# Building the third segment's output, and the last one's first octet, in the bank of P @ V instead of a bank borrowed from the maxima

## The chip, the cores and the metric

The kernel runs on one core of one Trainium2 chip. The metric is the device time in microseconds (us). The time before is the median of three runs; beside it stands one profiled execution, from which every duration in this document before the prediction is taken.

## The reference

Two attention layers over the same 2048 tokens are mixed by a gate that depends on the token:

```python
x = A_x                                             # 2048 x 512
g = sigmoid((x * gate_w).sum(-1, keepdims=True))
a = A_ref(x, A_wqkv, A_wo)       # 32 heads of 16, softmax over all 2048 keys, then @ wo
b = B_ref(x, B_wq, B_wk, B_wv, B_wo, B_beta)
                                 # 4 segments of 512 tokens: causal softmax inside the segment,
                                 # plus a memory of earlier segments, then @ wo
return g * a + (1 - g) * b
```

Everything is float32. Both layers end in a product with a 512 x 512 matrix, so the output rows of one block of 128 tokens are a sum over 2 sides x 4 groups of 8 heads ("octets"), each with K = 128.

## The kernel before, in words

**Segments and units.** The four segments of 512 query tokens are numbered 0 to 3. A unit is one side, four heads and one segment: side A has 8 units in each segment (all 2048 keys), side B also 8 (the segment's own keys). Units alternate A, B, A, B; at the very end the order is B, A (line 100). An A unit has 64 slots, a B unit 10. A slot is one 128 x 512 tile of scores: one matmul into a bank of `st` (line 615), one exp on ScalarE into a tile `p` (line 638). There are 2368 slots, 592 in a segment, 74 in a pair of an A and a B unit.

**Two passes.** The scores are made twice. 96 slots ahead of its exp (LEAD), a first product of the same size is made into a bank of `sm` (line 205) and VectorE takes the row maxima of it (line 220; B's diagonal blocks go by ScalarE, GpSimd and VectorE, lines 231 to 235). The maxima are transposed (line 195) and loaded into two rows of the q tile, so that the second product has them subtracted already. In every slot one score matmul and one matmul for the maxima are issued, in alternating halves of the array's rows. The last 96 slots have no maxima beside them.

**Banks of PSUM in the main stage (lines 567 to 573).** Three banks `st` for scores; four banks `sm0` to `sm3` for products of maxima, handed round through the list `free` (line 840); one bank `ops`, in which P @ V of one unit at a time is summed.

**Bursts.** The loop at line 831 issues three slots, then one burst of other work on TensorE. P @ V comes from a queue (line 598), into which four pieces of 128 columns go when their four exps are issued. A burst takes 3 pieces from it, or 4 when more than 6 wait (`MOST + (len(queue) > 6)`, line 851); neighbours of one tile are joined in a matmul of up to 512 columns, one for each of the four heads in its own 32 columns of the array (line 671). A piece is 128 columns. When a unit's last piece is done, ScalarE copies `ops` out (line 675) and a DMA stores it. The tiles `p` are six (`NP`, line 39), four slots each; a score may only be written over a tile whose P @ V is issued (line 609).

**The output product.** `octet` (line 701) loads eight stored heads back, scales them by the reciprocal of the sum, the gate and so on, some 28 slots later. `piece` (line 744) multiplies one scaled octet of one side with one quarter of the columns of `wo`: four matmuls of 128 columns side by side in the array. A block of 128 tokens has 32 pieces. They are issued in three ways:

- Segments 0 and 1 (`SHARED`): at the end of each A unit of the *next* segment, `half_block` (line 774) queues 16 pieces, half of the columns of one block, summed in `ops` itself. As long as there are any, a burst issues four of them in place of P @ V (line 847). ScalarE then copies 128 x 256 out (line 783).
- Segment 2: `block_fill` (line 758) takes a bank out of `free` and fills it with 32 pieces, one in each burst, behind that burst's P @ V (lines 856 to 859). Four blocks in turn; line 790 copies each out. The first octet of segment 3 (`keep`, 8 pieces a block, from slot nS - 208) goes the same way into tiles `part` (line 799). While a block is under way three banks are left for the maxima.
- The rest of segment 3 (`close`, line 818): one bank for each of the four blocks, two pieces in a burst once the maxima are over, `part` added at the end (line 868).

Pieces of the last two ways leave out a burst in which maxima are transposed (line 853).

Of the kernel before, what the change touches and what calls it, by code (L numbers as in the profile page):

```python
# [10 lines left out]
F32 = mybir.dt.float32  # L11
# [8 lines left out]
D = 512  # L20
# [3 lines left out]
NCH = S // CH  # L24
KT = D // 128
NG = 8
NO = 4
# [9 lines left out]
BURST = 3  # L37
MOST = 3
NP = 6
SHARED = (0, 1)  # L40
GAP = {"A": 3, "B": 5}
MASK_T = 8
LATE_T = 8
# [5 lines left out]
def gated_mix(ctx, tc, x, xT, wqkv, a_wo, b_wq, b_wk, b_wv, b_wo, beta, gate_w, out):  # L49
    nc = tc.nc  # L50
# [56 lines left out]
    seg_end = {(s, c): max(end[s, g, c] for g in range(NG)) for s in "AB" for c in range(NCH)}  # L107
    nS = len(slots)
# [4 lines left out]
    for k in range(NU):  # L113
# [4 lines left out]
        for p in range(64 + 10 * len(bs)):  # L118
            r = (len(maxs) + 1) % 2
            i = (p - start) // apart  # L120
# [131 lines left out]
    def run_todo(m):  # L252

        for e in [e for e in todo if e[0] <= m]:
            todo.remove(e)
            e[1]()
# [22 lines left out]
    with ExitStack() as p0:  # L279
# [22 lines left out]
        def post(slots, place, f):  # L302
            posted.setdefault((now[0] + slots, place), []).append(f)
# [163 lines left out]
        def mem_q(o, c, pq):  # L467
            nps = me_ps.tile([128, CH], F32, tag="me", name="num")
            nc.tensor.matmul(nps, mbd[o].rearrange("p e h -> p (e h)"), pq, start=True, stop=True)  # L469
            am = wk.tile([128, CH], F32, tag="am", name="am", bufs=1)  # L470
            nc.scalar.copy(am, nps)
            nc.sync.dma_start(numd[c][:, o], am)
            pqs.append(pq)
            if o == NO - 1:
                post(1, 1, lambda: mem_den(c))
# [13 lines left out]
        def mem_k(o, c, pk, vs):  # L489
            tps = me_ps.tile([128, 4, 128], F32, tag="me", name="tps")  # L490
            for b in range(4):
                nc.tensor.transpose(tps[:, b], pk[:, b * 128:(b + 1) * 128], identf)
            pt = wk.tile([128, 4, 128], F32, tag="pt", name="pt", bufs=1)
            nc.scalar.copy(pt, tps)
            post(0, 3, lambda: mem_k2(o, c, pt, vs))
# [36 lines left out]
        for c in range(NCH):  # L532
            for o in range(NO):
                then = (lambda pq, o=o, c=c: post(1, 1, lambda: mem_q(o, c, pq))) if c else None
# [5 lines left out]
            for o in range(NO):  # L540
                then = (lambda pk, o=o, c=c, vs=vs: post(1, 1, lambda: mem_k(o, c, pk, vs))) if c + 1 < NCH else None
# [24 lines left out]
    fr = ctx.enter_context(tc.tile_pool(name="fr", bufs=1, reuse_waits="tile"))  # L566
# [4 lines left out]
    banks = [sm_ps.tile([128, CH], F32, name=f"sm{i}") for i in range(4)]  # L571

    ops = o_ps.tile([128, CH], F32, name="ops")
# [4 lines left out]
    def load_wo(side, w):  # L578
        wos[side] = wo.tile([128, NO, D], F32, name=f"wo{side}")
        nc.sync.dma_start(wos[side], w.rearrange("(o p) d -> p o d", p=128))  # L580
# [17 lines left out]
    queue = []  # L598
# [51 lines left out]
    def some_values(n, most):  # L650

        while queue and most and queue[0][0] <= n:
            _, u, i = queue.pop(0)
            most -= 1
            side, g, c = u
            w = 1
            while (queue and most and queue[0][0] <= n and queue[0][1] == u and (i + w) // 4 == i // 4
                   and (side == "A" or PIECES[i + w][0] == PIECES[i][0])):
                queue.pop(0)
                most -= 1  # L660
                w += 1
            p = pt_[u, i // 4]
            if side == "A":
                c0 = q0 = 128 * (i % 4)
                v = vt[u][:, i // 16, i // 4 % 4]
            else:
                b, c0, q0 = PIECES[i]
                v = vt[u][:, b]
            done = i + w == SLOTS[side]
            for h in range(4):  # L670
                nc.tensor.matmul(ops[32 * h:32 * h + 17, q0:q0 + 128 * w], v[:, 17 * h:17 * h + 17], p[:, h, c0:c0 + 128 * w],  # L671
                                 start=(i == 0), stop=done, tile_position=(0, 32 * h))
            if done:
                raw = ob.tile([128, CH], F32, tag="o", name="oraw")
                nc.scalar.copy(raw, ops)
                nc.sync.dma_start(od[side, c][4 * g:4 * g + 4].rearrange("h r t -> (h r) t"), raw)
                stored.add(u)
                if side == "B" and c and g % 2 == 0:
                    octet("M", g // 2, c, n + 4)
                if (side, g ^ 1, c) in stored and u != ("A", NG - 1, NCH - 1):  # L680
                    octet(side, g // 2, c, n + 8)
                if side == "A" and c - 1 in SHARED:
                    shared.extend(half_block(c - 1, g // 2, g % 2))
                return


# [11 lines left out]
    def at(n, f):  # L698
        beside.setdefault(n, []).append(f)
# [44 lines left out]
    def piece(ps, side, o, c, b, j, start, stop):  # L744

        assert (side, o, c) in scaled
        for t in range(4):
            nc.tensor.matmul(ps[32 * t:32 * t + 32, 128 * (j % (ps.shape[1] // 128)):128 * (j % (ps.shape[1] // 128)) + 128],  # L748
                             held[side, c][:, o, 128 * b + 32 * t:128 * b + 32 * t + 32], wos[side][:, o, 128 * j:128 * j + 128],
                             start=start, stop=stop, tile_position=(0, 32 * t))  # L750

    def out_rows(c, b):
        return out[c * CH + b * 128:c * CH + (b + 1) * 128, :]

    fill = []
    lent = {}

    def block_fill(n, octets, c, b, then):

        ks = [(side, o) for o in octets for side in "AB"]  # L760
        for i in range(4 * len(ks)):
            def f(i=i):
                if i == 0:
                    lent[c, b] = free.pop(0)
                ps = banks[lent[c, b]]
                piece(ps, *ks[i // 4], c, b, i % 4, i == 0, i == 4 * len(ks) - 1)
                if i == 4 * len(ks) - 1:
                    then(ps)
                    free.append(lent[c, b])
            fill.append((n, f))  # L770

    shared = []

    def half_block(c, b, half):

        ps = ops[:, 0:256]
        ks = [(side, o) for o in range(NO) for side in "AB"]
        for i in range(16):
            def f(i=i):
                piece(ps, *ks[i // 2], c, b, 2 * half + i % 2, i == 0, i == 15)  # L780
                if i == 15:
                    t = fr.tile([128, D], F32, tag="res", name="res", bufs=2)
                    nc.scalar.copy(t[:, 0:256], ps)
                    nc.sync.dma_start(out_rows(c, b)[:, 256 * half:256 * half + 256], t[:, 0:256])
            yield f

    def leave(c, b):
        def then(ps):
            t = fr.tile([128, D], F32, tag="res", name="res", bufs=2)
            nc.scalar.copy(t, ps)  # L790
            nc.sync.dma_start(out_rows(c, b), t)
        return then

    part = {}

    def keep(b):
        def then(ps):
            part[b] = fr.tile([128, D], F32, tag=f"part{b}", name="part")
            nc.scalar.copy(part[b], ps)
        return then  # L800

    for u in units:
        at(max(0, first[u] - 30), lambda u=u: load_v(u))
    at(100, lambda: load_wo("A", a_wo))
    at(180, lambda: load_wo("B", b_wo))
    last = NCH - 1
    for c in range(NCH):
        if c < last and c not in SHARED:
            for b in range(4):
                block_fill(seg_end["A", c] + 24, range(NO), c, b, leave(c, b))  # L810
    for b in range(4):
        block_fill(nS - 208, range(1), last, b, keep(b))

    free = list(range(4))
    closing = [(side, o) for o in range(1, NO) for side in "BA"]
# [14 lines left out]
    n = 0  # L830
    while n < nS or queue or beside or filled[0] < len(fill):
        for f in beside.pop(n, []):
            f()
        if n < nS:
            score_part(n)
        m = n + LEAD
        if m < nS:
            loads(m + PRE)

            def bank():  # L840
                i = free.pop(0)
                free.append(i)
                return banks[i]
            max_part(m, bank)
        run_todo(m)
        if n % BURST == BURST - 1 or n >= nS:
            if shared:
                for _ in range(4):
                    shared.pop(0)()
            else:  # L850
                some_values(n, MOST + (len(queue) > 6) if n < nS else 8)

            if any(e[0] < m + 1 for e in late):
                run_late(st_ps, "st", m + 1)
            else:
                for _ in range(1 if m < nS else 2):
                    if filled[0] < len(fill) and fill[filled[0]][0] <= n:
                        fill[filled[0]][1]()
                        filled[0] += 1
        n += 1  # L860
    octet("A", NO - 1, last, None, vector=True)
    assert len(stored) == len(units)
    for b in range(4):
# [3 lines left out]
        t = fr.tile([128, D], F32, tag="res", name="res", bufs=2)  # L867
# [37 lines left out]
```

## Time and profile before

| | |
|---|---|
| median of 3 runs | 1941.87 us (1939.02 to 1943.77) |
| the profiled execution's own time | 1940.47 us |
| its span, first to last instruction | 1938.8 us |
| clock granted to TensorE, mean over the span | 0.993 |

By the starts of the score matmuls of line 615, the main stage goes from 345.1 us to 1913.4 us after the span's start. Segment 0's slots begin at 345.1, segment 1's at 727.4, segment 2's at 1109.8, segment 3's at 1493.6. "Stretch" below means a part of the span between two such times. Durations of neighbouring matmuls overlap in the profile, because matmuls are pipelined; the distance between the starts of two instructions is therefore used as the price of what lies between.

### The profile page before, as it was taken

Reading aid. Unit: us, or ns where it says so; the run is one execution under the profiler, and the core shown is the slowest. Engines: PE = TensorE matmul, PEld = TensorE weight load, DVE = VectorE, ACT = ScalarE, POOL = GpSimd, SP = SyncE. Lnnn points to the kernel's source line nnn. Section 1 sums busy time; section 2 is a strip of 40 time slices with the busy share of each in tenths; the row PEclk is TensorE's granted clock in tenths of the full one; section 3 lists DMA queues with packets and bytes.
Section 4 is the critical chain, followed back from the end, with each engine's and each line's share of the span. In section 5 each row is a group of like instructions: output and inputs, shape, how many; then the busy total and the mean of one; then the engine's idle time right before and its main releaser. Section 6 shows DMA issues by size and latency. Waiting matters only on the chain.

```text
span 1938.8 us, 44063 instructions
## 1 busy us (share of the span) xinstructions
PE 1897.4 (98%) x17009; PEld 993.5 (51%) x17009; DVE 1611.9 (83%) x2768; ACT 1467.0 (76%) x2859; POOL 281.7 (15%) x497
## 2 busy tenths in 40 slices
PE   7999999999999999999999999999999999999997
PEld 6888766444444444444444444444444455555545
DVE  4235687899999999999999999999999889889810
ACT  3234432788888888888888888888888787878874
POOL 3000000211111111121111111111111111111210
PEclk9999999899999999999999999999999999999999
DMA  6667645434233334343444344434334333333211
GB/s 204 204 228 254 201 155 166 114 101 133 85 107 84 107 85 119 91 117 91 118 93 116 103 105 104 104 105 107 105 104 105 101 93 102 101 105 96 80 53 40
DMA packets 123632, 227.16 MB, mean 117 GB/s; under 512 B 35064, under 2 KB 48920, under 8 KB 122912
## 3 DMA queue, kind: packets, MB, share of 16 engines
q1 hardware_dynamic: 121840, 223.24, 41.0%
q8 instruction: 135, 2.21, 0.5%
q0 software_dynamic: 1296, 0.59, 0.2%
q14 instruction: 73, 0.60, 0.1%
q10 hardware_dynamic: 288, 0.52, 0.1%
HBM read 155.52 MB, written 67.52 MB: 115 GB/s over the span
## 4 chain that ended last, share of the span: by engine, by line
PE 89%; DMA 3%; ACT 3%; DVE 3%; issue 1%; POOL 0%; SPq 0%; ACTq 0%; POOLq 0%; DVEq 0%
PE ops L671 30%; PE st L615 27%; PE sm L205 14%; PE pr L312 11%; PE ops L748 3%; PE sm L748 2%; ACT p L638 2%; DVE pm L220 1%; DMA qdA<-q 1%; PE num L469 1%; DMA kdB<-q 1%; PE mt_ps L195 1%; ACT dg L231 1%; PE mps L500 0%; DMA qdB<-q 0%
## 5 line engine op out<-in xcount | busy, mean ns | idle before, releaser
L638 ACT ACTIVATE p<-st 128x512 f32<-128x512 f32 x2304 | 1219.5, 605 | 205.8 <-PE sm L205 168.7
L220 DVE TENSOR_REDUCE pm<-sm 128x1 f32<-128x512 f32 x2048 | 1286.5, 682 | 94.1 <-PE sm L205 71.3
L205 PE MATMUL sm<-kA,qA 48*128 48x512 f32 x2048 | 757.7, 450 | 1.3 <-DVE pm L220 1.3
L615 PE MATMUL st<-qA,kA 50*128 50x512 f32 x2048 | 702.9, 439 | 7.8 <-ACT p L638 7.1
L671 PE MATMUL ops<-p,vA 128*17 128x512 f32 (+2 forms) x4912 | 561.2, 529 | 0.0
L615 PEld LDWEIGHTS st<-qA,kA 50*128 50x128 f32 x2048 | 336.1, 186 | 412.6 <-ACT p L638 336.9
L205 PEld LDWEIGHTS sm<-kA,qA 48*128 48x128 f32 x2048 | 338.3, 185 | 37.7 <-DVE pm L220 22.9
L205 PE MATMUL sm<-kB,qB 48*128 48x128 f32 (+2 forms) x896 | 171.5, 295 | 0.6 <-DVE pmB L241 0.5
L671 PEld LDWEIGHTS ops<-p,vA 128*17 128x17 f32 x4912 | 81.7, 95 | 165.0 <-issue 153.9
L205 PEld LDWEIGHTS sm<-kB,qB 48*128 48x128 f32 x896 | 135.0, 188 | 10.6 <-DVE pm L220 2.6
L232 POOL TENSOR_SCALAR_AFFINE_SELECT dg<-dg 128x512 f32<-128x512 f32 x128 | 81.2, 637 | 301.2 <-ACT dg L231 299.6
L615 PE MATMUL st<-qB,kB 50*128 50x384 f32 (+3 forms) x512 | 120.9, 342 | 3.3 <-ACT p L638 2.4
L360 DVE TENSOR_TENSOR q<-pr,q 128x512 fp32r<-128x512 f32 x64 | 44.0, 687 | 90.8 <-ACT q L353 78.3
L353 ACT CAST q<-pr 128x512 fp32r<-128x512 f32 x64 | 37.5, 585 | 99.3 <-PE pr L312 63.6
L188 POOL CAST ms<-nm 128x16 fp32r<-128x16 f32 x64 | 12.6, 197 | 650.5 <-DVE nm L181 392.5
L615 PEld LDWEIGHTS st<-qB,kB 50*128 50x128 f32 x512 | 72.6, 186 | 66.3 <-ACT p L638 52.0
L619 POOL TENSOR_SCALAR_AFFINE_SELECT p<-p 128x512 f32<-128x512 f32 x128 | 78.7, 634 | 95.6 <-ACT p L638 95.0
L671 PE MATMUL ops<-p,vB 128*17 128x512 f32 (+3 forms) x1024 | 89.2, 444 | 1.7 <-issue 1.5
L241 DVE TENSOR_REDUCE pmB<-sm 128x4 f32<-128x512 f32 x128 | 87.1, 681 | 1.2 <-PE sm L205 1.2
L235 DVE TENSOR_REDUCE pmB<-dg 128x4 f32<-128x512 f32 x128 | 86.7, 677 | 0.8 <-POOL dg L232 0.8
L231 ACT COPY dg<-sm 128x512 f32<-128x512 f32 x128 | 76.4, 597 | 1.8 <-DVE pmB L235 1.8
L722 DVE RECIPROCAL rec<-rec 128x32 f32<-128x32 f32 x44 | 15.1, 343 | 71.2 <-DMA rec<-odA 40.3
(129 smaller groups left out, 1567.5 us busy)
## 6 DMA issues: line engine op xcount, KB each, us to landing
kA<-kdA SPq DMA_DIRECT2D x256, 128.0 KB
vA<-vdA SPq DMA_DIRECT2D x32, 544.0 KB
kA<-kdA SPq DMA_DIRECT2D x256, 64.0 KB
qdA<-q SPq DMA_DIRECT2D x32, 256.0 KB
kdA<-q SPq DMA_DIRECT2D x32, 256.0 KB
qdB<-q SPq DMA_DIRECT2D x32, 256.0 KB
qA<-qdA SPq DMA_DIRECT2D x64, 128.0 KB
kdB<-q SPq DMA_DIRECT2D x32, 256.0 KB
```

The source lines that it names most:

```text
L205: nc.tensor.matmul(ps[:, n0:n0 + n], rows(qt[u][:, :, s * 128:(s + 1) * 128], h, 48), rows(k[:, :, k0:k0 + n], h, 48), start=True, stop=True)
L220: nc.vector.tensor_reduce(pm[:, h, s, kc:kc + 1], ps, axis=AX.X, op=ALU.max)
L231: nc.scalar.copy(dg, blocked(ps))
L232: nc.gpsimd.affine_select(out=dg, in_=dg, pattern=[[0, 4], [-1, 128]], base=0, channel_multiplier=1, compare_op=ALU.is_ge, fill=MASKED)
L235: todo.append((m + MASK_T, lambda: nc.vector.tensor_reduce(to, dg.rearrange("p (h s) t -> p h s t", h=2), axis=AX.X, op=ALU.max)))
L241: nc.vector.tensor_reduce(pm[:, 1, h, 3:7], blocked(ps), axis=AX.X, op=ALU.max)
L312: nc.tensor.matmul(ps, l(a, k), r(b, k), start=(n == 0), stop=(n == 11))
L615: nc.tensor.matmul(ps[:, n0:n0 + CH - q0], rows(k[:, :, b * 128:(b + 1) * 128], h, 50), rows(q[:, :, q0:], h, 50), start=True, stop=True)
L619: nc.gpsimd.affine_select(out=x, in_=x, pattern=[[0, 4], [1, 128]], base=0, channel_multiplier=-1, compare_op=ALU.is_ge, fill=0.0)
L638: nc.scalar.activation(p[:, h], ps, AF.Exp, scale=SCALE)
L671: nc.tensor.matmul(ops[32 * h:32 * h + 17, q0:q0 + 128 * w], v[:, 17 * h:17 * h + 17], p[:, h, c0:c0 + 128 * w], start=(i == 0), stop=done ...
L748: nc.tensor.matmul(ps[32 * t:32 * t + 32, 128 * (j % (ps.shape[1] // 128)):128 * (j % (ps.shape[1] // 128)) + 128], held[side, c][:, o, 12 ...
```

## The change

The whole of segment 2's output and the first octet of segment 3 leave the borrowed bank. `half_block`, `block_fill` and the numbers in `SHARED` become one generator `output(c, b, octets, cols, then)`, which sums in the first columns of `ops`, and a table `between` that says which unit's end starts which piece of output:

- at the end of each A unit of segments 1, 2 and 3 except the very last: half of the columns of one block of the segment before (16 pieces, four bursts of four), as segments 0 and 1 had it;
- at the ends of the first two B units of segment 3: one quarter each of the columns that the last A unit leaves over (8 pieces, two bursts);
- at the ends of the next four B units of segment 3: the first octet of one block of segment 3, all columns (8 pieces, two bursts), copied to `part`.

No bank is taken out of `free` any more before the closing pieces. A burst of P @ V now takes a fifth piece when more than 13 wait; this holds in all segments. `close` and the end of the kernel stay as they are.

```diff
-                if side == "A" and c - 1 in SHARED:
-                    shared.extend(half_block(c - 1, g // 2, g % 2))
+                if u in between:
+                    shared.extend(output(*between[u]))
...
-    def block_fill(n, octets, c, b, then):
-        ks = [(side, o) for o in octets for side in "AB"]
-        for i in range(4 * len(ks)):
-            def f(i=i):
-                if i == 0:
-                    lent[c, b] = free.pop(0)
-                ps = banks[lent[c, b]]
-                piece(ps, *ks[i // 4], c, b, i % 4, i == 0, i == 4 * len(ks) - 1)
-                if i == 4 * len(ks) - 1:
-                    then(ps)
-                    free.append(lent[c, b])
-            fill.append((n, f))
...
+    def output(c, b, octets, cols, then):
+        ps = ops[:, 0:128 * len(cols)]
+        ks = [(side, o, j) for o in octets for side in "AB" for j in cols]
+        for i, (side, o, j) in enumerate(ks):
+            def f(i=i, side=side, o=o, j=j):
+                piece(ps, side, o, c, b, j, i == 0, i == len(ks) - 1)
+                if i == len(ks) - 1:
+                    then(ps, c, b, cols)
             yield f
...
+    last = NCH - 1
+    between = {("A", g, c): (c - 1, g // 2, range(NO), range(2 * (g % 2), 2 * (g % 2) + 2), leave)
+               for c in range(1, NCH) for g in range(NG)}
+    del between["A", NG - 1, last]
+    for j in (2, 3):
+        between["B", j - 2, last] = (last - 1, 3, range(NO), (j,), leave)
+    for b in range(4):
+        between["B", b + 2, last] = (last, b, (0,), range(4), keep)
...
-    for c in range(NCH):
-        if c < last and c not in SHARED:
-            for b in range(4):
-                block_fill(seg_end["A", c] + 24, range(NO), c, b, leave(c, b))
-    for b in range(4):
-        block_fill(nS - 208, range(1), last, b, keep(b))
...
-                some_values(n, MOST + (len(queue) > 6) if n < nS else 8)
+                some_values(n, MOST + (len(queue) > 6) + (len(queue) > 13) if n < nS else 8)
```

More of the change, by code (lines that the diff above doesn't have):

```diff
@@ L39 @@
 NP = 6
-SHARED = (0, 1)
 GAP = {"A": 3, "B": 5}
@@ L755, in gated_mix @@
     fill = []
-    lent = {}
-    def block_fill(n, octets, c, b, then):
-        ks = [(side, o) for o in octets for side in "AB"]
-        for i in range(4 * len(ks)):
-            def f(i=i):
-                if i == 0:
-                    lent[c, b] = free.pop(0)
-                ps = banks[lent[c, b]]
-                piece(ps, *ks[i // 4], c, b, i % 4, i == 0, i == 4 * len(ks) - 1)
-                if i == 4 * len(ks) - 1:
-                    then(ps)
-                    free.append(lent[c, b])
-            fill.append((n, f))
@@ L772, in gated_mix @@
-    shared = []
[L774 to L784, printed above, removed]
-            yield f
@@ L787, in leave @@
[L787 to L792, printed above, removed]
-    part = {}
[L796 to L800, printed above, removed]
+    shared = []
+    def output(c, b, octets, cols, then):
[6 more added lines that the diff above has]
+                    then(ps, c, b, cols)
+            yield f
@@ new lines, in leave, with keep @@
+    def leave(ps, c, b, cols):
+        w, j0 = 128 * len(cols), 128 * cols[0]
+        t = fr.tile([128, D], F32, tag="res", name="res", bufs=2)
+        nc.scalar.copy(t[:, 0:w], ps)
+        nc.sync.dma_start(out_rows(c, b)[:, j0:j0 + w], t[:, 0:w])
+    part = {}
+    def keep(ps, c, b, cols):
+        part[b] = fr.tile([128, D], F32, tag=f"part{b}", name="part")
+        nc.scalar.copy(part[b], ps)
+    last = NCH - 1
+    between = {("A", g, c): (c - 1, g // 2, range(NO), range(2 * (g % 2), 2 * (g % 2) + 2), leave)
+               for c in range(1, NCH) for g in range(NG)}
@@ L805, in gated_mix @@
     at(180, lambda: load_wo("B", b_wo))
-    last = NCH - 1
-    for c in range(NCH):
-        if c < last and c not in SHARED:
-            for b in range(4):
-                block_fill(seg_end["A", c] + 24, range(NO), c, b, leave(c, b))
-    for b in range(4):
-        block_fill(nS - 208, range(1), last, b, keep(b))
     free = list(range(4))
```

## The prediction, made before the changed kernel was run

> **What bounds the kernel now.** The page comes first, then the span cut at the segments' borders.
>
> ```profile
> PE 1897.4 (98%) x17009; PEld 993.5 (51%) x17009; DVE 1611.9 (83%) x2768; ACT 1467.0 (76%) x2859; POOL 281.7 (15%) x497
> ...
> PEclk9999999899999999999999999999999999999999
> ```
>
> TensorE is busy almost everywhere, but its row counts pipelined matmuls; the stages say more. The view by stretches (columns: busy us of the engines, clock, DMA):
>
> ```profile
> core 0: us, PE busy (x) PEld busy (x) DVE busy (x) ACT busy (x) POOL busy (x), PEclk, DMA share, GB/s
> 345.00:727.40 382.40, 374.05 (x2981) 164.36 (x2982) 364.46 (x621) 333.78 (x660) 60.79 (x114) 0.98 0.38 101
> 727.40:1109.80 382.40, 380.14 (x3741) 177.41 (x3737) 368.11 (x632) 335.78 (x664) 65.20 (x112) 1.00 0.41 106
> 1109.80:1493.60 383.80, 381.07 (x3851) 178.62 (x3848) 370.09 (x635) 338.21 (x666) 67.46 (x114) 1.00 0.41 105
> 1493.60:1804.60 311.00, 308.98 (x3299) 158.48 (x3295) 278.50 (x469) 249.02 (x488) 46.41 (x79) 1.00 0.37 98
> 1804.60:1848.80 44.20, 43.52 (x484) 24.19 (x480) 38.09 (x66) 36.63 (x72) 11.36 (x17) 1.00 0.31 85
> 1848.80:1913.40 64.60, 63.96 (x834) 31.53 (x830) 1.30 (x6) 51.48 (x102) 9.53 (x15) 0.97 0.11 32
> 1913.40:1938.70 25.30, 15.09 (x405) 13.14 (x401) 4.00 (x7) 1.40 (x3) 0.00 (x0) 0.83 0.22 76
> ```
>
> The first three rows are segments 0, 1, 2; segment 3 takes 311.0 + 44.2 + 64.6 = 419.8, 36 more than segment 2, although its last 96 slots have no maxima. Segments 1 and 2, with 120 and 128 pieces of output in `ops`, take no more than 1.4 over segment 0, which has none. In segment 2 VectorE is busy 370.1 of 383.8 (96%); in the first stretch of segment 3, 278.5 of 311.0 (90%). The groups of those two stretches show its idle time (after the bar: busy, mean ns, idle before):
>
> ```profile
> L220 DVE TENSOR_REDUCE pm<-sm 128x1 f32<-128x512 f32 x382 | 242.6, 683 | 29.2 <-PE sm L205 23.2 <-PE st L615 5.1
> ```
> ```profile
> L220 DVE TENSOR_REDUCE pm<-sm 128x1 f32<-128x512 f32 x515 | 322.1, 681 | 13.0 <-PE sm L205 8.7 <-PE st L615 1.5
> ```
>
> Per maximum 76 ns in segment 3 (first line) against 25 in segment 2. Both engines have slack there, so the handover between them is what is late. A burst of segment 0, four banks:
>
> ```profile
> 605.49 1.05 PE L671 MATMUL ops<-p,vA 128*17 128x512 f32 x8
> 606.47 0.50 PE L615 MATMUL st<-qA,kA 50*128 50x512 f32 x1
> ...
> 607.38 0.84 PE L671 MATMUL ops<-p,vA 128*17 128x384 f32 x8
> 608.15 0.50 PE L615 MATMUL st<-qA,kA 50*128 50x512 f32 x1
> ```
>
> and two of segment 3, three banks:
>
> ```profile
> 1625.86 0.50 PE L615 MATMUL st<-qA,kA 50*128 50x512 f32 x1
> ...
> 1626.76 0.18 PEld L205 LDWEIGHTS sm<-kA,qA 48*128 48x128 f32 x1 [0.16 <-DVE pmB L245]
> ...
> 1627.19 1.05 PE L671 MATMUL ops<-p,vA 128*17 128x512 f32 x8
> ...
> 1628.06 0.40 PE L748 MATMUL sm<-woB,vB 128*32 128x128 f32 x8
> ...
> 1628.39 0.49 PE L615 MATMUL st<-qA,kA 50*128 50x512 f32 x1
> ...
> 1628.95 0.69 DVE L220 TENSOR_REDUCE pm<-sm 128x1 f32<-128x512 f32 x1 [0.46 <-PE sm L205]
> ...
> 1629.81 3.13 DVE L220 TENSOR_REDUCE pm<-sm 128x1 f32<-128x512 f32 x5
> ...
> 1630.48 0.50 PE L615 MATMUL st<-qA,kA 50*128 50x512 f32 x1
> ```
>
> Six score products take 606.47 to 607.38, 0.91. P @ V takes 0.98 for four pieces and 0.77 for three, so 0.21 to 0.22 a piece and 0.11 for the way back to scores. A piece of output costs the same: 1628.06 to 1628.39 is 0.33, way back included. Hence TensorE's price of a burst: 1.02 + 0.2175 for each piece of either kind; 1.89 with four, 2.11 with five, 1.68 with three. VectorE's price: the five reductions at 1629.81 come every (3.13 - 0.68) / 4 = 0.61, three in 1.84. With three banks the third product of maxima waits for a bank (1626.76), the six products take 1.33 (1625.86 to 1627.19) instead of 0.91 and the burst 2.53; then VectorE runs dry (0.46 at 1628.95), because TensorE could not get far enough ahead before P @ V and the piece.
>
> **The change part by part.** Counts are from the recorded order of both programs on TensorE.
>
> *The maxima keep four banks.* The pieces are moved, none is added or saved. The stretch 1493.6 to 1804.6 (146 bursts) has 444 pieces of P @ V and 138 of output before, 444 and 128 after; by the price above TensorE needs 146 x 1.02 + 582 x 0.2175 = 275 before and 273 after, and 12 transposes at the price of a lone piece (0.33) make these 279 and 277. What goes is the wait for a bank; next comes VectorE, whose 278.5 at segment 2's share (370.1 / 383.8) give 289. Five runs at B units in this stretch are new, and each waits for ScalarE to empty `ops`, as a run in segment 2 did:
>
> ```profile
> 1300.39 0.65 PE L748 MATMUL ops<-woA,vA 128*32 128x128 f32 x16 [0.47 <-ACT oraw L675]
> ...
> 1302.31 0.65 PE L748 MATMUL ops<-woA,vA 128*32 128x128 f32 x16
> ...
> 1303.32 0.50 PE L615 MATMUL st<-qA,kA 50*128 50x512 f32 x1
> ```
>
> A run's burst costs 1.01 here for its four pieces, 0.03 over a P @ V of four. 5 x 0.47 = 2.4, so I take 291 for the stretch: **-20**. Bounds: 277 (TensorE's need alone) and 299 (29 bursts of five, below, each 0.27 dearer than VectorE's 1.84, with no backlog to hide it).
>
> The Trainium skill, "TensorEngine Tiling (Array Packing)", section PSUM Bottleneck, speaks against a gain: packing the array speeds up TensorE but not the emptying of PSUM, which may then be the limit. By it alone the fourth bank would bring nothing and the stretch would stay at 311; VectorE's share of 90% there against 96% in segment 2 leaves room down to 289, so the rows decide for the gain.
>
> *1804.6 to 1848.8* (20 bursts, six of them runs): VectorE's 38.1 at the same share is 39.5, one B run 0.5: 40, **-4**. TensorE's need is 20 x 1.02 + 82 x 0.2175 = 38.
>
> *1848.8 to 1913.4*, hardly any maxima. Here 16 pieces arrive at the end of the last A unit but one: 16 x 0.2175 = 3.5 more for TensorE. They fall on its thinnest place:
>
> ```profile
> 1860.72 0.98 PE L615 MATMUL st<-qB,kB 50*128 50x256 f32 x4
> ...
> 1865.41 0.73 PE L615 MATMUL st<-qB,kB 50*128 50x512 f32 x3
> ```
> ```profile
> 1858.70:1862.00 3.30, 2.71 (x18) 1.44 (x14) 0.00 (x0) 3.20 (x9) 1.19 (x3) 0.99 0.22 83
> 1862.00:1865.40 3.40, 3.38 (x25) 1.20 (x25) 0.00 (x0) 1.00 (x2) 1.07 (x2) 0.50 0.02 6
> 1922.00:1926.80 4.80, 0.06 (x4) 0.00 (x0) 0.00 (x0) 0.00 (x0) 0.00 (x0) 1.00 0.27 96
> 1926.80:1933.60 6.80, 5.60 (x108) 5.05 (x112) 2.26 (x4) 0.00 (x0) 0.00 (x0) 0.50 0.14 52
> ```
>
> One burst there takes 4.69, with the clock at half for 3.4 after TensorE was busy 2.71 of 3.30. A run fills the gap; if it also keeps the clock up, up to 4.69 - 2.11 = 2.6 comes back. I take **+1**, bounds -2 and +3.5. The Trainium skill, "TensorE: Matmul & The Clock Gate", section What's actually happening, halves the clock after an idle window of about 3.4 us. By that rule the half clock here has another cause than this thin place, the run does not remove it, and the term would be 3.5 - 2.6 + 1.7 (half of the 3.4) = +2.6; the row (no idle window ahead of it) does not agree with the rule.
>
> *The fifth piece* also changes segments 1 and 2: 20 and 25 bursts of five, for fewer of four. The columns are the same, so TensorE's need is; but a burst of 2.11 leaves VectorE 0.27 short. Bounds: 0, if its backlog covers it (four maxima in four banks are 2.4), and 45 x 0.27 = 12. These bursts follow the runs, where VectorE's idle time is small already (25 ns a maximum in segment 2), so a part is covered: **+3**.
>
> *Copies and stores.* In place of four copies of 512 columns and four stores, segment 2's output has seven of 256 and two of 128:
>
> ```profile
> L783 ACT COPY res<-ops x16: 372/373/375, 779.3 to 1497.6; 128x256 f32<-128x256 f32 x16
> ```
> ```profile
> L790 ACT COPY res<-sm x4: 586/587/590, 1575.2 to 1798.3; 128x512 f32<-128x512 f32 x4
> ```
>
> 7 x 0.373 + 2 x under 0.373 against 4 x 0.587 is at most 1.0 more on ScalarE, busy 249 of 311: hidden by its idle time, and worth 1.0 without it. Behind a store on SyncE's queue stand the next loads of q and k, 20 slots early (about 13), against a wait of one copy: **0**. The added waits stand on TensorE alone; behind them are the next score products, whose price is in the 0.47.
>
> *The end.* After the last score 38 closing pieces are left instead of 48, but the end hangs on the last unit's copy, store, reload and scaling:
>
> ```profile
> 1916.04 0.59 ACT L675 COPY oraw<-ops 128x512 f32<-128x512 f32 x1 [1.53 <-PE ops L671]
> ...
> 1918.39 3.68 PE L748 MATMUL sm<-woB,vB 128*32 128x128 f32 x128
> ...
> 1927.25 0.69 DVE L734 TENSOR_TENSOR vA<-vA,inv 128x512 f32<-128x512 f32 x1 [5.26 <-DMA inv<-rdA]
> ```
>
> TensorE is done at 1922.07 and waits until 1928; it will wait 2.2 longer. The last 16 pieces run at half clock either way (0.50 from 1926.8): **0**, plus or minus 1.7, half a clock window.
>
> Sum: -20 - 4 + 1 + 3 + 0 = -20. From the profiled execution's 1940.5 (1938.8 of span and 1.7 around it) that is **1920**; this execution is 1.4 under the median of 1941.87, which I leave in the range.
>
> **The rivals.**
>
> *Wide bursts eat the gain.* VectorE runs dry behind bursts of five wherever they stand: 299 in the first stretch, +12 in segments 1 and 2, +3.5 near the end: -12 - 4 + 3.5 + 12 = 0, so 1928 (half of it) to 1940. For: 0.46 of idle time at 1628.95 after such a burst; against: that was with three banks.
>
> *The bank was not the limit.* If the 311 come from 72 bursts of four plus one, at 2.11, nothing changes: 1940. Against: the need of 279, which has those bursts in it, leaves 32 unexplained, and the six products took 1.33 for 0.91.
>
> *Slower: exps wait for tiles of p.* With 24 pieces a pair in runs, P @ V falls further behind: at most 23 pieces wait, where six tiles hold 24, and 21 before. The tile about to be used is the last one freed in 50 bursts of segments 1 to 3 after, 31 before. If ScalarE then stands until P @ V has run, each costs between nothing and a P @ V of four, 0.98: 50 x 0.98 = 49 against -20 is 1969. It decides from 0.4 a burst. Against: segments 1 and 2 have 30 such bursts already and keep 1.94 a burst.
>
> **How the numbers follow.** Forecast, 1909 to 1927: 0.72. Wide bursts, 1928 to 1934: 0.12. No change, 1935 to 1946: 0.07. Slower by tiles of p: 0.07. More than forecast, under 1909 (the first stretch at 277): 0.02. A measurement of this kernel can tell some 0.3% (5.8) from no change; so faster 0.86, same 0.07, slower 0.07. The range 1909 to 1934 holds 0.84.
>
> **What would show it.** Right: the stretch of 146 bursts from the first score of segment 3 takes 286 to 295, the idle time of line 220's reductions falls there from 76 to about 25 ns each, and segments 1 and 2 stay within 5 of 382. Wrong: that idle time stays; or segments 1 and 2 grow by over 5 (the fifth piece); or exps wait for P @ V at runs (tiles of p).

## The result and the profile after

The changed kernel takes 1924.7 us (median of four runs, 1923.64 to 1926.57) against 1940.44 for the kernel before on the same chip: 0.9917 of it, 95% interval 0.9905 to 0.993. It is faster by 15.7 us, which is under 1% but outside the noise: the interval does not reach 1. The profiled execution took 1924.45, its span is 1922.7.

The stretches of the changed kernel, cut at the same slots as those of the kernel before (columns as there; line numbers are one lower):

```profile
344.60:727.50 382.90, 376.22 (x2981) 167.04 (x2982) 364.52 (x621) 333.83 (x660) 60.83 (x114) 0.98 0.36 101
727.50:1112.60 385.10, 382.40 (x4060) 187.82 (x4057) 369.36 (x632) 335.85 (x663) 65.02 (x111) 1.00 0.39 105
1112.60:1500.00 387.40, 383.98 (x4291) 192.37 (x4288) 371.79 (x635) 338.23 (x666) 67.43 (x114) 1.00 0.38 105
1500.00:1789.40 289.40, 287.94 (x3459) 146.23 (x3455) 275.88 (x469) 249.86 (x494) 46.06 (x78) 1.00 0.37 105
1789.40:1831.70 42.30, 41.91 (x580) 24.75 (x576) 37.56 (x64) 36.68 (x72) 11.58 (x17) 1.00 0.34 93
1831.70:1896.40 64.70, 64.39 (x969) 33.87 (x965) 1.55 (x7) 50.87 (x101) 9.53 (x15) 1.00 0.11 34
1896.40:1922.70 26.30, 11.72 (x325) 10.05 (x321) 4.00 (x7) 1.45 (x3) 0.00 (x0) 0.84 0.22 73
```

| part | before | after | difference | predicted |
|---|---|---|---|---|
| segment 0 | 382.4 | 382.9 | +0.5 | 0 |
| segments 1 and 2 | 766.2 | 772.5 | +6.3 | +3 |
| 146 bursts of segment 3 | 311.0 | 289.4 | -21.6 | -20 |
| the next 20 bursts | 44.2 | 42.3 | -1.9 | -4 |
| to the last score | 64.6 | 64.7 | +0.1 | +1 |
| end | 25.3 | 26.3 | +1.0 | 0 |

With 0.5 less ahead of segment 0 (345.1 to 344.6) this is the 16.1 between the two spans. The large term is where it was looked for. In the 146 bursts the group of the reductions of maxima reads (busy, mean ns, idle before):

```profile
L219 DVE TENSOR_REDUCE pm<-sm 128x1 f32<-128x512 f32 x382 | 240.5, 682 | 12.3 <-PE sm L204 8.1 <-PE st L614 1.8
```

12.3 of idle time instead of 29.2, 32 ns a maximum instead of 76. The wait for a bank itself stands in the weight loads of the products of maxima (line 205, 204 after), with TensorE's idle time ahead of them and what ended it, before first, then after:

```profile
L205 PEld LDWEIGHTS sm<-kA,qA 48*128 48x128 f32 x382 | 64.2, 184 | 11.0 <-DVE pm L220 8.3 <-ACT dg L231 0.3 <-DVE pmB L245 0.3
```
```profile
L204 PEld LDWEIGHTS sm<-kA,qA 48*128 48x128 f32 x382 | 63.4, 185 | 0.5 <-DVE pm L219 0.2
```

11.0, most of it ended by a reduction that frees a bank, falls to 0.5. The other side of the account stands in segments 1 and 2, where only the fifth piece is new. Four bursts of five in a row, from TensorE's timeline of the changed kernel:

```profile
1311.80 0.50 PE L614 MATMUL st<-qA,kA 50*128 50x512 f32 x1
...
1312.75 1.27 PE L670 MATMUL ops<-p,vB 128*17 128x512 f32 x16
1313.95 0.50 PE L614 MATMUL st<-qA,kA 50*128 50x512 f32 x1
...
1314.86 1.27 PE L670 MATMUL ops<-p,vB 128*17 128x256 f32 x24
1316.06 0.50 PE L614 MATMUL st<-qA,kA 50*128 50x512 f32 x1
...
1318.22 0.50 PE L614 MATMUL st<-qA,kA 50*128 50x512 f32 x1
...
1320.33 0.50 PE L614 MATMUL st<-qA,kA 50*128 50x512 f32 x1
```

From one first score to the next: 2.15, 2.11, 2.16, 2.11, close to the price of 2.11 that the prediction had.

### The profile page after: what moved, and what is told of

Its sections match the earlier page's. It is cut to its first block, busy times and chain, and to the rows that moved or that the text cites. A ratio compares the mean times of both kernels' runs of the same rounds, so it can differ in the third digit from the quotient of the medians.

```text
span 1922.7 us, 46247 instructions
## 1 busy us (share of the span) xinstructions
PE 1878.9 (98%) x18081; PEld 1007.5 (52%) x18081; DVE 1612.1 (84%) x2768; ACT 1467.3 (76%) x2864; POOL 281.4 (15%) x497
## 4 chain that ended last, share of the span: by engine, by line
PE 91%; DMA 3%; ACT 3%; DVE 2%; issue 1%; SPq 0%; ACTq 0%; DVEq 0%
PE ops L670 30%; PE st L614 28%; PE sm L204 13%; PE pr L311 11%; PE ops L747 5%; ACT p L637 2%; PE sm L747 1%; DMA qdA<-q 1%; PE num L468 1%; ACT dg L230 1%; DMA kdB<-q 1%; PE mt_ps L194 1%; DVE pm L219 1%; PE mps L499 0%; DMA qdB<-q 0%
## 5 line engine op out<-in xcount | busy, mean ns | idle before, releaser
L670 PE MATMUL ops<-p,vA 128*17 128x512 f32 (+3 forms) x5784 | 558.9, 473 | 0.0
L670 PEld LDWEIGHTS ops<-p,vA 128*17 128x17 f32 x5784 | 107.5, 95 | 196.7 <-issue 177.4
L670 PE MATMUL ops<-p,vB 128*17 128x128 f32 (+3 forms) x1224 | 84.1, 394 | 1.5 <-issue 1.5
```

## The experiments

The theory: a borrowed bank of maxima costs the time, because TensorE then cannot run far enough ahead of VectorE. Its rival: the single piece behind P @ V in nearly every burst. Beside them, the fifth piece takes part of the gain back. Each stretch below is the one of 146 bursts from the first score of segment 3, unless said otherwise, and comes from one profiled execution. A version that was run once has no interval. Where two versions issue the same instructions in segments 1 and 2 or in the 146 bursts, the lengths of these stretches agree within 0.2.

**The bank taken away without its pieces.** The changed kernel, with a bank withheld:

```diff
         m = n + LEAD
+        if n == 1790:
+            kept = free.pop(0)
+        if n == nS - LEAD:
+            free.append(kept)
```

> The changed kernel, but one of the four banks of maxima is taken out of the rotation from slot 1790 until the maxima are over, and used for nothing: the loan of the kernel before without its pieces, which stay in the bank of P @ V. Theory (the missing bank is the cost): the stretch of 146 bursts goes from 289 back to 303 to 315, and the time to 1938 to 1950. Rival (it was the single piece behind P @ V in nearly every burst that cost the time, and runs of four are the gain): the stretch stays at 288 to 292 and the time within 1922 to 1929.

Measured: 1940.86 (one run; before 1940.33 beside it), stretch 304.2. Views by stretch and by group:

```profile
1501.10:1805.30 304.20, 302.77 (x3457) 159.20 (x3453) 278.98 (x469) 250.79 (x494) 46.14 (x78) 1.00 0.35 100
```
```profile
L219 DVE TENSOR_REDUCE pm<-sm 128x1 f32<-128x512 f32 x382 | 242.8, 684 | 22.3 <-PE sm L204 15.4 <-PE st L614 4.4
```

With nothing else altered, the bank is worth 14.8 in this stretch and the idle time of the reductions goes from 12.3 to 22.3 (29.2 before). TensorE's wait for a bank is back at its size of before:

```profile
L204 PEld LDWEIGHTS sm<-kA,qA 48*128 48x128 f32 x381 | 63.7, 184 | 11.5 <-DVE pm L219 7.9 <-DVE pmB L244 0.6 <-ACT dg L230 0.6
```

The rival as an explanation of the whole is refuted; but 304 is at the low edge of what was expected and 6.8 short of the 311 before, so the bank is not all of it.

**The loan alone.** The kernel before, with `block_fill` lending the bank as before but issuing no piece of segment 2's output (that output is left out):

```diff
-                piece(ps, *ks[i // 4], c, b, i % 4, i == 0, i == 4 * len(ks) - 1)
+                if c == last:
+                    piece(ps, *ks[i // 4], c, b, i % 4, i == 0, i == 4 * len(ks) - 1)
```

> The kernel before, with the bank lent as before but the pieces of segment 2's output left out (its rows of the output are not the reference's). Theory (the bank): with six score products at 1.33 in place of 0.91, bursts of four at 2.31, of three at 2.1 and of one at 1.66 average 2.09, so the stretch of 146 bursts takes 295 to 306, 5 to 16 under the 311 of before. Rival (the piece in each burst): the stretch falls to segment 0's pace of 47.3 a pair, 280 to 284.

Measured: 1925.88, stretch 296.5:

```profile
1495.10:1791.60 296.50, 293.50 (x2275) 133.44 (x2271) 276.57 (x469) 247.53 (x488) 46.37 (x79) 1.00 0.37 102
```

That is inside the theory's 295 to 306, at its low end, and far from the rival's 280 to 284.

**Neither loan nor pieces.** The kernel before, without segment 2's output at all:

```diff
-        if c < last and c not in SHARED:
+        if c < last and c not in (0, 1, 2):
...
-        block_fill(nS - 208, range(1), last, b, keep(b))
+        block_fill(2214, range(1), last, b, keep(b))
```

> The kernel before, with neither loan nor pieces for segment 2's output (its rows of the output are not the reference's); the first octet of segment 3 still starts at the slot where it started before. Both theories: the stretch of 146 bursts at segment 0's pace, 280 to 284. It is the floor from which the loan (the run with the loan alone) and the pieces in runs (the changed kernel, 289) are counted.

Measured: 1912.72, stretch 280.2:

```profile
1497.10:1777.30 280.20, 276.02 (x2259) 120.61 (x2255) 272.16 (x469) 243.89 (x484) 46.09 (x78) 1.00 0.39 105
```
```profile
L220 DVE TENSOR_REDUCE pm<-sm 128x1 f32<-128x512 f32 x382 | 238.0, 682 | 7.3 <-PE sm L205 5.0 <-PE st L615 1.1
```

That is at the low edge of the 280 to 284 that both expected. The five runs of this stretch form a table ("no pieces" means none of segment 2's output; 8 pieces of segment 1's output are in the stretch in every run):

| | no pieces | pieces in runs of four in `ops` | a piece behind P @ V |
|---|---|---|---|
| four banks of maxima | 280.2 | 289.4 (changed) | not tried: no bank for it |
| three banks | 296.5 | 304.2 | 311.0 (before) |

Read down, the loan costs 16.3 without pieces and 14.8 with them. Read across with three banks, the pieces cost 14.5 one by one and 7.7 in runs. So of the 21.6 that the change gains here, about 15 are the bank. The other 7 or so, a third, are what is left: the pieces in runs instead of one by one (the rival), ten pieces fewer in the stretch (2.2 by the price of a piece), no handing over of the borrowed bank from block to block, and against these the bursts of five, which only the changed kernel and the run with three banks have. No run separates these four in this stretch, and the prediction did not either.

**Without the runs at B units.** The changed kernel, minus the two quarters and the first octet of segment 3 that B units start (missing from the output):

```diff
-    for j in (2, 3):
-        between["B", j - 2, last] = (last - 1, 3, range(NO), (j,), leave)
-    for b in range(4):
-        between["B", b + 2, last] = (last, b, (0,), range(4), keep)
+    for b in range(4):
+        part[b] = fr.tile([128, D], F32, tag=f"part{b}", name="part")
+        nc.vector.memset(part[b], 0.0)
```

> The changed kernel without the runs at the ends of B units of segment 3 (one quarter of a block of segment 2 twice, and the first octet of segment 3: these sums are missing from the output). The stretch of 146 bursts has ten bursts of pieces less, 88 pieces in place of 128. Theory (TensorE has room, VectorE sets the pace, and pieces cost little but through bursts of five): the pace of segments 1 and 2 of the changed kernel, 48.3 a pair, so 285 to 287 against 289.4. Rival (each run costs its full price, 8 pieces and a wait of 0.47 for the bank, 2.2 each): 278 to 279.

Measured: 1921.82, stretch 285.4:

```profile
1502.10:1787.50 285.40, 283.27 (x3083) 139.12 (x3079) 275.09 (x469) 247.52 (x489) 46.09 (x78) 1.00 0.38 105
```

That is in the theory's 285 to 287. Five runs of 8 pieces cost 4.0, 0.8 each, where their full price would be 2.2: pieces in runs are mostly paid for by time in which TensorE would have waited for VectorE. By the order of issue the edit also leaves 18 bursts of five in the stretch instead of 29; at the 0.14 each that the next run gives, 1.5 of the 4.0 are those (an estimate).

**The fifth piece only in segment 3.**

```diff
-                some_values(n, MOST + (len(queue) > 6) + (len(queue) > 13) if n < nS else 8)
+                some_values(n, MOST + (len(queue) > 6) + (len(queue) > 13 and n >= nS // 4 * 3) if n < nS else 8)
```

> The changed kernel, but the fifth piece of P @ V in a burst is allowed only from the first slot of segment 3 on. Segments 1 and 2 then have no burst of five. Theory (a burst of five costs VectorE some 0.14 us each, 20 and 25 of them): segments 1 and 2 go back from 385.1 and 387.4 to 382.3 and 383.9, the stretch of 146 bursts from the first score of segment 3 stays at 289, and the time falls by 6 to about 1918. Rival (the growth of segments 1 and 2 comes from something else in the change, say where code or data lie): they stay at 385 and 387 and the time at 1924.

Measured: 1919.3 (median of four, 1916.94 to 1922.84) against 1940.33, ratio 0.9896 (0.9879 to 0.9912). Its segments 1 and 2 and the stretch:

```profile
730.80:1113.10 382.30, 380.07 (x3739) 177.29 (x3735) 368.11 (x631) 335.77 (x663) 65.34 (x111) 1.00 0.40 106
1113.10:1496.90 383.80, 381.09 (x3851) 178.49 (x3849) 370.19 (x635) 338.23 (x666) 67.77 (x114) 1.00 0.39 105
1496.90:1786.20 289.30, 287.83 (x3457) 146.22 (x3453) 275.95 (x469) 249.77 (x494) 46.17 (x78) 1.00 0.39 105
```

382.3 and 383.8 are the kernel before to 0.1; the stretch is the changed kernel to 0.1. The 6.3 of segments 1 and 2 are the fifth piece alone: 2.8 for 20 bursts of five and 3.6 for 25, 0.14 each in both; the rival is refuted. This is the fastest version here with its full output; its median is 5.4 under the changed kernel's, although the two intervals of the ratios overlap a little (up to 0.9912 here, from 0.9905 there), so the stretches carry that verdict. Inside segment 3 the fifth piece is needed: in the order of issue without it the queue outgrows the six tiles `p` (worked out from the order, not run).

**More matmuls, same columns.** A fifth piece also breaks the joined matmuls of 512 columns. On the version just shown, in segments 1 and 2:

```diff
-                   and (side == "A" or PIECES[i + w][0] == PIECES[i][0])):
+                   and (side == "A" or PIECES[i + w][0] == PIECES[i][0])
+                   and not (nS // 4 <= n < nS // 4 * 3 and side == "A" and i % 4 == 0)):
```

> The kernel with the fifth piece in segment 3 alone, but in segments 1 and 2 the first of four joined pieces of P @ V is issued as a matmul of its own, so that each burst holds the same columns in more matmuls (303 and 301 groups of four heads in place of 175 and 173; the changed kernel has 215 and 228, bursts of five among them). Theory (width: what cost the changed kernel 2.8 and 3.5 in these segments are the bursts of five): 382 to 383.5 and 384 to 385 for the two segments, as without the split. Rival (the number of matmuls: 40 and 55 more groups cost 2.8 and 3.5, 0.07 each): 128 more groups in each make 391 and 393.

Measured: 1920.85, segments at 382.7 and 384.3:

```profile
730.80:1113.50 382.70, 380.43 (x4763) 205.01 (x4759) 368.18 (x631) 335.83 (x663) 65.14 (x111) 1.00 0.40 106
1113.50:1497.80 384.30, 381.58 (x4877) 206.46 (x4875) 370.32 (x635) 338.33 (x666) 67.56 (x114) 1.00 0.38 106
```

1024 and 1026 more matmul records, 0.4 and 0.5 more time: the number of matmuls is not the cost, which leaves the width of the burst.

**A fifth bank for the maxima, taken from the scores.** On the version with the fifth piece in segment 3 alone:

```diff
-    st_ps = ctx.enter_context(tc.tile_pool(name="st_ps", bufs=3, space=PSUM, reuse_waits="tile"))
+    st_ps = ctx.enter_context(tc.tile_pool(name="st_ps", bufs=2, space=PSUM, reuse_waits="tile"))
...
-    banks = [sm_ps.tile([128, CH], F32, name=f"sm{i}") for i in range(4)]
+    banks = [sm_ps.tile([128, CH], F32, name=f"sm{i}") for i in range(5)]
```

> The kernel with the fifth piece in segment 3 alone, with one bank moved from the scores to the maxima: two for scores, five for maxima. Theory (a bank more for maxima lets TensorE run further ahead of VectorE, but VectorE already works near its pace of 0.61 a maximum with four, and two banks hold up the exps, of which three come in a burst): segments 1 and 2 at 390 to 410, the time 1935 to 1990. Rival (maxima are what any further bank helps, as from three to four): segments at 376 to 380, the time under 1910.

Measured: 2590.38 (median of four, 2571.78 to 2623.2), ratio 1.3279 (1.3231 to 1.3328), segments 1 and 2 at 549.7 and 518.5. The direction was expected, the size was not. From its timeline in segment 2:

```profile
1500.30 0.50 PE L614 MATMUL st<-qA,kA 50*128 50x512 f32 x1 [0.48 <-ACT p L637]
...
1501.70 0.50 PE L614 MATMUL st<-qA,kA 50*128 50x512 f32 x1
...
1502.89 0.50 PE L614 MATMUL st<-qA,kA 50*128 50x512 f32 x1 [0.44 <-ACT p L637]
```

Three scores of a burst no longer fit ahead of the exps: the third one (at 1500.30, and of the next burst at 1502.89) waits for ScalarE, a burst takes 2.59, and everything in line behind that score waits too. Over the whole run, which has some 790 bursts, score matmuls waited for ScalarE this often (us in total, times, longest):

```profile
PE st L614 <- ACT p L637: 298.2, 727, 1.2
```

298.2 is less than half of the 671 by which this version is longer than the one it was made from. The mean granted clock of its profiled execution is 0.896 as well, against 0.991 to 0.995 in the runs of the changed kernel.

## Why the prediction was right

It said 1920 and it was 1924.7, inside the range and on the side forecast. Against the profiled execution the sum was 3.9 too hopeful: 3.3 in segments 1 and 2, 2.1 in the 20 bursts and 1.0 at the end, less 1.6 and 0.9 where the measured term was the better one.

Of the signs that it named, the stretch (289.4) lies in the 286 to 295, and the idle time fell to 32 ns, not quite to about 25. One sign of being wrong came up: segments 1 and 2 grew by 6.3 together, over the 5 that were to speak against the fifth piece, and segment 2 alone, at 387.4, is 5.4 over 382. Point by point:

- *The maxima keep four banks:* the wait for a bank went, as said, and the size is near, -21.6 for -20, but the size is in part luck. It put the whole difference down to the bank; the table gives the bank about 15 and the rest of the change about 7. It took 289 for what VectorE needs; without pieces the same reductions went through in 280.2. So 289 is not VectorE's limit but its pace with pieces beside it: the 96.4% came from segment 2, which has such pieces too. And the bursts of five, which it left to the bounds, are in the 289.4. A busy share hides them (95.3% here), because in the rows shown of before a reduction's row lasts 682 ns while five in a row came every 610 ns: by its rows VectorE can look busy throughout in a burst of 1.84 and in one of 2.05 (3 x 0.682).

  By the Trainium skill's page "TensorEngine Tiling (Array Packing)", section PSUM Bottleneck, taken alone the stretch would have stayed at 311. 289.4 says that here the emptying of PSUM still had room, and 280.2 without pieces that it had more.
- *The fifth piece:* the term that was mis-sized most, +6.3 for +3. A burst of five took 2.11 to 2.16, as priced some 0.27 over VectorE's pace, and 0.14 of that was paid, half, where the prediction had assumed a quarter. That VectorE's backlog covers the other half is argued, not shown.
- *1804.6 to 1848.8:* -1.9 for -4. The stretch was priced at segment 2's share of VectorE; it ended at 37.6 busy of 42.3, 89%. It carries the maxima of two B units, whose diagonal blocks go by ScalarE first, busy 36.7 of 42.3. That this is why the forecast was missed is argued from those rows and was not tried. With the bank withheld this part took 43.8, so most of the 1.9 that came is the bank again.
- *1848.8 to 1913.4:* +0.1 for +1, near, but by luck. The run fell into the gap as expected: of the bursts there none takes over 2.7, where one took 4.69. The granted clock stayed up at that place:

```profile
1839.70:1851.00 11.30, 10.99 (x216) 7.69 (x212) 0.00 (x0) 9.24 (x21) 3.12 (x5) 1.00 0.08 29
```

  By the clock gate rule of the Trainium skill ("TensorE: Matmul & The Clock Gate", What's actually happening), as the prediction had applied it, this part would have taken 2.6 more; it took 0.1 more.

  The clock stays up there without the run too. The version with the loan alone issues the same instructions as the kernel before in this part and has no run there, and no half clock fell into it either:

```profile
1835.70:1898.70 63.00, 62.36 (x834) 31.09 (x829) 1.35 (x6) 51.48 (x102) 9.53 (x15) 1.00 0.11 33
```

  It took 63.0, and the version with neither loan nor pieces 63.0 too; the longest burst was 3.1 in both. So the run costs some 1.7 (64.7 against 63.0), and the half-clock window of the kernel before had cost 1.6, about half of its 3.4; the two happen to cancel. Such windows move from run to run. In segment 0, whose instructions are the same in both kernels, one came at 537.6 in the kernel before and at 630.9 in the changed one (before first, then after):

```profile
537.60:541.00 3.40, 3.40 (x19) 1.20 (x15) 2.34 (x5) 1.84 (x5) 1.20 (x3) 0.50 0.61 149
```
```profile
630.90:634.30 3.40, 3.40 (x18) 1.31 (x15) 1.93 (x5) 1.71 (x5) 1.81 (x3) 0.50 0.48 130
```

- *Copies and stores, the end:* the end took 1.0 longer, within the 1.7 allowed. ScalarE's extra copies show in its busy time (249.9 for 249.0); that they cost time is not seen.
- *The rivals:* wide bursts did eat part of the gain: 6.3 in segments 1 and 2, half of the bound of 12. At the same 0.14, the 29 of the stretch would be some 4 more, an estimate that no run isolates. That the bank was not the limit is refuted by the bank withheld. That exps wait for tiles of `p` did not happen: in the stretch of the changed kernel what ended ScalarE's idle time ahead of an exp of line 637 was line 204 (83 times) or line 614 (12 times), never P @ V; and in segments 1 and 2 taking the fifth piece away lengthens the queue and shortens the time.

## What to carry to other kernels

Count how many results the fast engine can leave for the slow one before it turns to other work: lending one of four such buffers cost 5% of the stretch, though TensorE's need as priced was 279 of the 311 and VectorE was busy 90%. Work that must go into the same queue costs least where the fast engine would have waited anyway, here in runs of four that take the place of equal work. A rule that lets a backlog shrink faster cost time here, because it made single steps longer than the slow engine's pace; allow it only where the buffers force it.

## What the runs showed of the hardware that was not expected

- Splitting P @ V's matmuls of 512 columns into 128 and 384 is close to free: some 1024 more matmul records a segment for 0.4 to 0.5 us.
- Taking the third bank from the scores makes the whole kernel a third longer (2590 for 1919). The waits of the score matmuls add up to 298.2; the granted clock of 0.896 is part of the rest, and the shares were not separated.
- Half-clock windows of about 3.4 us move from run to run in the same instructions; one of them had cost the kernel before 1.6 in its last 64.6, and looked like the work of a thin place.
